# Linear attention and a gated feed-forward on one core: batch 0 by pairs of heads, its key products on two 64x64 tiles, and one transpose issued ahead of a load

## The chip, the cores and the metric

One core of one Trainium2 chip. The metric is device time in microseconds (us), the median of several executions. The profile gives a span of a little less: 284.0 us for an execution of the kernel before that was timed at 285.86 us.

## The reference

```python
q, k, v: (8 batches, 8 heads, 576 positions, 64) float32
q_s = softmax(q, over the 64)          k_s = softmax(k, over the 576 positions)
kv  = einsum('bhsd,bhse->bhde', k_s, v)            # 64x64 per head
x   = einsum('bhsd,bhde->bhse', q_s, kv)           # then (4608 tokens, 512)
h   = x @ w_in                                     # w_in  (512, 2048)
out = (h * sigmoid(beta * h)) @ w_out              # w_out (2048, 512)
```

The expert part (two products per token) is nearly all of TensorE's work. Attention is small, but the expert part of batch 0 can't begin before attention of batch 0 has delivered its transposed output, called XT below.

## The kernel before

The kernel records operations in one order; each engine runs its own in that order, and waits on semaphores only where data or a buffer demand it. So the place of an operation in the text is its place in its engine's queue. The eight heads go as four pairs (hp 0 to 3), two heads on 128 partitions. The 576 positions are cut in 512 (slabs t = 0 to 7, one for each batch) and 64 "remainders", which together make slab 8.

For a pair, the two heads' key exps lie on the diagonal of a block form (EK), zeros beside them, so that one 128-wide product serves both heads. Batch 0 before:

```python
def exp_kh(b, hp, n, e_):          # one head of n pairs: 64 partitions, ScalarE
    ... e.activation(o, a, ACT.Exp) ...
def ksum(b, hp, kb):               # 9 products, 1 column: the sums of key exps
    for j in range(NG):
        mm(PS[kb][:, hp:hp + 1], EK.., ones.., ...)
def kv_mm(b, hp, bk, n, w=D):      # 9 products, 64 or 65 columns: keys x values
    for j in range(NG):
        mm(PS[bk][:, VW * n:VW * n + w], EK.., VB.., ...)

load_main("qf", ...); load_k(0, 4)            # later: load_v(0, 4), then w_in
exp_q(0)
for hp in range(2):
    exp_kh(0, hp, 1, hp); exp_kh(0, hp, 1, 1 - hp)
exp_kh(0, 2, 2, 0); exp_kh(0, 2, 2, 1)        # pairs 2 and 3 together
...
cast_v(0, 0); cast_v(0, 1); cast_v(0, 2, ACTE); cast_v(0, 3)   # VB, default GpSimd
cast_win(0, 2, POOL); cast_win(0, 3, POOL); cast_win(1, 0, POOL)
...
out_now(0, 0, 0, ACTE)             # product QT x KVD, then the copy to XT (here ScalarE)
```

After the products come a reciprocal and two multiplies on VectorE (KVD, the normalised 64x64 blocks), one product with the transposed queries (QT) and the copy to XT. With XT, the first expert product starts: 64 matmuls "XT, WIN" for slab 0, then 64 "WOUT, GT".

`warm(...)` are filler products whose results nobody reads. The end of slab 0's work:

```python
                norm_rem(0)      # VectorE: query remainders of batches 0 and 1 normalised
                store(0)         # SyncE queue: output of slab 0
                load(3)          # SyncE queue: q, k, v of batch 3, query remainders of 2 and 3
                tr_dma(0)        # SyncE queue: DMA transpose EQR -> QTR
```

QTR is used in the second half of slab 1, by eight small products (remainders of batches 0 and 1).

The softmax here doesn't subtract the row's maximum and nothing guards it: scores larger than these inputs give would overflow.

Of the kernel before, what the change touches and what calls it, by code (L numbers as in the profile page):

```python
# [14 lines left out]
D = 64  # L15
# [28 lines left out]
class Program:  # L44
# [12 lines left out]
    def add(self, eng, fn, r=(), w=(), bank=(), slot=None, after=()):  # L57
        op = Op(eng, fn, slot)
        op.pos = len(self.ops)
        deps = op.deps  # L60
        deps.extend(after)
        for k in r:
            deps.extend(self.writer.get(k, ()))
            self.readers.setdefault(k, []).append(op)
        for k in w:
            for d in self.readers.get(k, ()):
                if d is not op and not self._same(d, op):
                    deps.append(d)
            for d in self.writer.get(k, ()):
                if not self._same(d, op):  # L70
                    deps.append(d)
            self.readers[k] = []
            self.writer[k] = [op]
        for k in bank:
            t = self.touch.setdefault(k, {})
            for e, d in t.items():
                if e != eng:
                    deps.append(d)
            t[eng] = op
        if eng == POOL and slot is None:  # L80
            if self.pool is not None:
                deps.append(self.pool)
            self.pool = op
        self.ops.append(op)
        return op
# [71 lines left out]
def bass_efficient_attn_shen__then__act_swish_beta_kernel(  # L157
# [12 lines left out]
    with ExitStack() as es:  # L170
# [57 lines left out]
        def homes_vk(i):  # L228
            add(POOL, lambda e: e.memset(VB[i][:, :, :, D:VW], 1.0), w=[("vone", i)])
            for e_ in range(2):  # L230
                z = KVD[i][64 * e_:64 * e_ + 64, :, 64 * (1 - e_):64 * (2 - e_)]
                add(POOL, lambda e, z=z: e.memset(z.bitcast(F32), 0.0), w=[("kvz", i, e_)])
# [36 lines left out]
        def load_k(b, split=1, cs=None, engs=(SP,)):  # L269
            load_pairs("kf", kt_h, KF, b, split, cs, engs)  # L270

        def load_v(b, split=1, cs=None):
            load_pairs("vf", vt_h, VF, b, split, cs)

        def load(b):
# [7 lines left out]
        load_main("qf", qt_h, QF, 0, 4, None, (SP, ACTE))  # L283
        add(ACTE, lambda e: e.dma_start(BT[:, :], bass.AP(beta_h, 0, [[512, 4], [1, 512]])),
            w=["bt"], slot="bt")
        load_k(0, 4)
        add(ACTE, lambda e: e.activation(DUMMY[:, 0:1], WARM[:, 0:1], ACT.Exp), r=["warm"],
            w=["dummy"])

# [20 lines left out]
        def exp_kh(b, hp, n, e_):  # L310
            i = b % 2
            o = bass.AP(EK[i], 64 * e_ * NHP * NG * 128 + hp * NG * 128 + 64 * e_,
                        [[NHP * NG * 128, 64], [128, NG * n], [1, 64]])
            a = bass.AP(KF[i], 64 * e_ * NHP * KW + hp * KW,
                        [[NHP * KW, 64], [64, NG * n], [1, 64]])
            hps = range(hp, hp + n)
            add(ACTE, lambda e: e.activation(o, a, ACT.Exp),  # L317
                r=[("kf", i, h) for h in hps], w=[("ek", i, h, e_) for h in hps])

        def exp_qr(pi):  # L320
            i = pi % 2
# [37 lines left out]
            rot[0] += 1  # L359
            return pool[rot[0] % len(pool)]  # L360

        def mm(o, l, r_, start, stop, r=(), w=(), bk=0, tr=False):
            if tr:
                add(PE, lambda e: e.transpose(o, l, r_), r=r, w=w, bank=[bk])  # L364
            else:
                add(PE, lambda e: e.matmul(o, l, r_, start=start, stop=stop), r=r, w=w, bank=[bk])  # L366

        def t_steps(b, hps, pool=MB, eng=DVE):
            i = b % 2
# [19 lines left out]
        def kv_rows(b, hp, j):  # L389
            i = b % 2  # L390
            return (EK[i][:, hp, j, :], VB[i][:, hp, j, :],
                    [("ek", i, hp, 0), ("ek", i, hp, 1), ("ekz", i, 0), ("ekz", i, 1)],
                    [("vb", i, hp, 0), ("vb", i, hp, 1)], [("vone", i)])
# [103 lines left out]
        def warm(n, bk, long=False):  # L497
            for _ in range(n):
                if long:
                    mm(PS[bk][:, :], bass.AP(XT8, 0, [[NM * SM, 128], [1, 256]]).bitcast(F32),  # L500
                       bass.AP(XT8, 0, [[NM * SM, 128], [1, 1024]]).bitcast(F32), True, True,
                       r=["xw"], w=[("ps", bk)], bk=bk)
                else:
                    mm(PS[bk][:, :], WARM[:, 0:128], WARM[:, :], True, True, r=["warm"],
                       w=[("ps", bk)], bk=bk)



        def ksum(b, hp, kb):
            for j in range(NG):  # L510
                l, r_, ke, kv, ko = kv_rows(b, hp, j)
                mm(PS[kb][:, hp:hp + 1], l, r_[:, D:D + 1], j == 0, j == NG - 1, r=ke + ko,
                   w=[("ps", kb)], bk=kb)

        def ksum_inv(b, kb, hp0, n, c0, step):
            i = b % 2
            s_ = bass.AP(PS[kb], c0, [[512, 128], [step, n]])
# [3 lines left out]
        def kv_mm(b, hp, bk, n, w=D):  # L521
            for j in range(NG):
                l, r_, ke, kv, ko = kv_rows(b, hp, j)
                mm(PS[bk][:, VW * n:VW * n + w], l, r_[:, 0:w], j == 0, j == NG - 1,
                   r=ke + kv + ko, w=[("ps", bk)], bk=bk)

        def out_now(b, hp, bk, eng):
            i = b % 2
# [31 lines left out]
        def load_win(c, m=0, nm=NM):  # L560
            a = bass.AP(win_h, m * 128 * DFF + 512 * c, [[DFF, 128], [128 * DFF, nm], [1, 512]])
            add(SP, lambda e: e.dma_start(STAGE[c][:, m:m + nm, :], a), w=SKEY[c][m:m + nm],
                slot=f"win{c}{m}")
# [27 lines left out]
        homes_ek(0, 0)  # L591
        homes_ek(0, 1)
        homes_vk(1)
        warm(3, 0, True)
        exp_q(0)
        for hp in range(2):
            exp_kh(0, hp, 1, hp)
            exp_kh(0, hp, 1, 1 - hp)
        exp_kh(0, 2, 2, 0)
        exp_kh(0, 2, 2, 1)  # L600
        norm_main(0, 0, 1)
        norm_main(0, 1, 1, POOL)
        go(t_steps(0, (0,), (3,)))
        turn_beta()
        warm(1, 0, True)
        norm_main(0, 2, 1, POOL)
        norm_main(0, 3, 1)
        go(t_steps(0, (1,), (4,)))
        ksum(0, 0, KB)
        load_v(0, 4)  # L610
        for c in range(4):
            for m in range(0, NM, 1 if c < 2 else 2):
                load_win(c, m, 1 if c < 2 else 2)
        cast_v(0, 0)
        cast_v(0, 1)
        cast_v(0, 2, ACTE)
        cast_v(0, 3)
        cast_win(0, 2, POOL)
        cast_win(0, 3, POOL)
        cast_win(1, 0, POOL)  # L620
        warm(1, 0, True)
        go(t_steps(0, (2,), (5,)))
        ksum(0, 1, KB)
        ksum_inv(0, KB, 0, 2, 0, 1)
        warm(1, 0)
        kv_mm(0, 0, 7, 0)
        kvd(0, 0, 7, 0)
        go(t_steps(0, (3,), (6,)))
        kv_mm(0, 1, 1, 0)
        kvd(0, 1, 1, 0)  # L630

        orot = [0]

# [27 lines left out]
                tick()  # L661

        FIRST = (16, 5)
        out_now(0, 0, 0, ACTE)
        cast_win(0, 0, DVE)
        kv_mm(0, 2, 7, 0, D + 1)
        ksum_inv(0, 7, 2, 1, D, 1)
        kvd(0, 2, 7, 0)
        cast_win(0, 1, DVE)
        out_now(0, 1, 6, ACTE)  # L670
        at = by_m(0, 0, 4)
        kv_mm(0, 3, 1, 0, D + 1)
        at(0)
        out_now(0, 2, 0, ACTE)
        ksum_inv(0, 1, 3, 1, D, 1)
        kvd(0, 3, 1, 0)
        at(1)
        out_now(0, 3, 7, DVE)
        read_beta()
        add(ACTE, lambda e: e.activation(DUMMY[:, 1:2], WARM[:, 0:1], ACT.Silu), r=["warm"],  # L680
            w=["dummy"])
# [72 lines left out]
        for t in range(NSLAB):  # L754
# [48 lines left out]
            if t == 0:  # L803
                load_qrem(0)
                load(2)
                scale_wout(0)
                scale_wout(4)
                exp_q(1, 0, 2)
                norm_main(1, 0, 1)
                scale_wout(8)  # L810
                norm_main(1, 1, 1, POOL)
                exp_q(1, 2, 2)
                exp_kh(1, 0, 2, 0)
                exp_kh(1, 0, 2, 1)
                norm_main(1, 2, 1, POOL)
                norm_main(1, 3, 1)
                scale_wout(12, 2)
                for hp in range(NHP):
                    cast_v(1, hp, POOL if hp else ACTE)
                pass2_group(0, (0, 1, 2, 3), (3, 4, 5, 6), tick)  # L820
                while todo:
                    todo.pop()[1]()
                at = by_m(1, 0, FIRST[1])
                o2_evac(0, 2, 5, ACTE)
                exp_qr(0)
                add(ACTE, lambda e: e.activation(DUMMY[:, 2:3], WARM[:, 0:1], ACT.Silu),
                    r=["warm"], w=["dummy"])
                at(0, 0, 3)
                out_now(1, 2, 7, DVE)
                at(1, 0, 3)  # L830
                go(kv_steps(1, (3,), (0,)))
                at(0, 3)
                at(1, 3)
                out_now(1, 3, 7, DVE)
                at(2)
                at(3)
                o2_evac(0, 3, 6, DVE)
                norm_rem(0)
                store(0)
                load(3)  # L840
                tr_dma(0)
                continue
            nb = [t + 2] if t + 2 < B else []
            if t == 1:
# [62 lines left out]
```

## Time and profile before

| | before |
|---|---|
| time | 285.6 us, median of 3 |
| span, TensorE busy | 284.0 us, 276.1 us (97%) |
| first expert product starts | 13.91 us |
| WOUT products start | 28.45 us |
| products on QTR start | 68.98 us |

First the view of TensorE's waits, kernel before. Columns: who waited and for whom, total us, how often, the longest.

```profile
PE PS L366 <- DVE XT L219: 1.5, 1, 1.5
PE PS L366 <- DMA QTR<-EQR: 1.1, 1, 1.1
PE PS L366 <- DVE KVD L403: 0.7, 1, 0.7
PE PS L366 <- DVE WOUT L555: 0.2, 1, 0.2
```

The first is the very beginning. The others are all the waits that this view lists in 284 us. The largest of them is for the transposed remainders. Its timeline (start, duration, engine, line, operation, tiles, count, idle before it and who ended that):

```profile
65.79 2.11 PE L366 MATMUL PS<-WOUT,GT 128*128 128x512 bf16 x8
68.98 0.26 PE L366 MATMUL PS<-QTR,KVD 128*128 128x64 bf16 x3 [1.09 <-DMA QTR<-EQR]
```

The SyncE queue of the same kernel, in order of time:

```profile
49.27 0.36 SPq L716 DMA_DIRECT2D out_dram<-O2S  x1
49.67 0.44 SPq L249 DMA_DIRECT2D QF<-in_q_dram  x1
...
53.58 6.86 SPq L266 DMA_DIRECT2D QRF<-in_q_dram  x2
60.48 3.98 SPq L456 DMA_TRANSPOSE QTR<-EQR  x1
```

VectorE had the remainders ready at 50.9 us, but the transpose is issued at 60.48, because load(3) is ahead of it: its last two issues alone hold the queue for 6.86 us. It lands 8.5 us after its issue, as the view by tile says:

```profile
DMA to landing us min/median/max: 8.5/8.5/8.5
```

The view of stretches, kernel before, says why it lands so late (the columns after the stretch are busy us and counts of each engine, then the granted clock, the share of the DMA engines, GB/s):

```profile
4.00:16.00 12.00, 11.33 (x98) 6.47 (x98) 9.49 (x27) 9.59 (x15) 6.72 (x11) 1.00 1.03 368
16.00:28.00 12.00, 11.94 (x56) 5.79 (x55) 5.90 (x17) 9.68 (x16) 2.97 (x4) 1.00 1.04 396
```

The DMA engines are full (share 1.0) in these stretches, as they are up to 64 us. A transfer issued then lands when those ahead of it have passed: all 95 transfers of the SyncE queue landed in their order of issue. And TensorE is nearly full too. The start, on which most of the change works, is this part of ScalarE's timeline:

```profile
7.41 4.90 ACT L317 ACTIVATE EK<-KF 64x576 bf16<-64x576 f32 x6 [0.90 <-DMA KF<-in_k_dram]
12.34 0.67 ACT L351 CAST VB<-VF 128x576 bf16<-128x576 f32 x1
12.92 0.58 ACT L530 CAST XT<-PS 128x512 bf16<-128x512 f32 x1
```

Key exps fill ScalarE from 7.4 to 12.3 us, and only then come the third V cast and the first copy of XT.

### The profile page before, as it was taken

How to read it: one execution, taken by the hardware profiler on the slowest of the kernel's cores; microseconds unless marked ns; L12 is line 12 of the kernel's file. 1: busy time of each engine (PE TensorE's matmuls, PEld its weight loads, DVE VectorE, ACT ScalarE, POOL GpSimd, SP SyncE). 2: the span in 40 equal slices, each digit the busy share in tenths (PEclk: the TensorE clock that was granted, in tenths of full speed). 3: DMA queues.
4: the chain of work that ended last, by engine and by line, in shares of the span. 5: the costliest groups of instructions: out<-in, count | busy, mean ns of one | idle time of the engine just before them, and what ended most of it. 6: DMA issues, size and time to landing. Idle time of an engine off the chain costs nothing.

```text
span 284.0 us, 3884 instructions
## 1 busy us (share of the span) xinstructions
PE 276.1 (97%) x1559; PEld 136.3 (48%) x1589; DVE 117.2 (41%) x218; ACT 178.9 (63%) x243; POOL 38.5 (14%) x57
## 2 busy tenths in 40 slices
PE   7999999998999999999999999999999999999995
PEld 3644454444455445544454445444554444444443
DVE  4864786126791248114741564054804300110012
ACT  5978688989867935796479737892660076018500
POOL 6522041127031122100140000000000000000000
PEclk9999999999999999999999999999999999999999
DMA  7999999999999998207980033002600030012022
GB/s 242 376 392 398 390 370 314 403 383 170 359 296 271 354 312 306 39 16 242 370 132 1 0 150 74 2 1 88 152 2 0 0 150 0 0 45 105 0 74 74
DMA packets 41466, 50.07 MB, mean 176 GB/s; under 512 B 20324, under 2 KB 28772, under 8 KB 40296
## 3 DMA queue, kind: packets, MB, share of 16 engines
q1 hardware_dynamic: 40496, 48.77, 54.3%
q10 hardware_dynamic: 952, 1.06, 1.1%
q8 instruction: 12, 0.20, 0.3%
q14 instruction: 6, 0.05, 0.0%
HBM read 36.71 MB, written 9.44 MB: 162 GB/s over the span
## 4 chain that ended last, share of the span: by engine, by line
PE 94%; DMA 3%; issue 1%; ACT 0%; DVE 0%
PE PS L366 93%; DMA QTR<-EQR 3%; PE PS L364 1%; ACT GT L642 0%; DVE XT L219 0%; DVE O2S L731 0%; DVE KVD L403 0%; ACT L295 0%
## 5 line engine op out<-in xcount | busy, mean ns | idle before, releaser
L642 ACT ACTIVATE GT<-PS,BETA 128x512 bf16<-128x512 f32 x144 | 96.8, 689 | 79.1 <-PE PS L366 79.1
L366 PE MATMUL PS<-WOUT,GT 128*128 128x512 bf16 (+2 forms) x579 | 131.4, 373 | 0.8 <-DVE WOUT L555 0.2
L366 PE MATMUL PS<-XT,WIN 128*128 128x512 bf16 x561 | 131.2, 379 | 0.5
L366 PEld LDWEIGHTS PS<-XT,WIN 128*128 128x128 bf16 x576 | 60.1, 106 | 59.3 <-POOL WIN L566 0.5
L366 PEld LDWEIGHTS PS<-WOUT,GT 128*128 128x128 bf16 x592 | 55.2, 98 | 62.3 <-ACT GT L642 0.4
L710 DVE COPY O2S<-PS 128x512 f32<-128x512 f32 x33 | 22.7, 687 | 107.7 <-PE PS L366 107.7
L366 PE MATMUL PS<-VB,EK 128*128 128x65 bf16 (+2 forms) x306 | 35.8, 191 | 1.0 <-DVE KVD L403 0.7
L351 POOL CAST VB<-VF 128x576 bf16<-128x576 f32 x30 | 22.7, 756 | 79.5 <-PE PS L366 49.9
L307 ACT ACTIVATE EK<-KF 64x1152 bf16<-64x1152 f32 x24 | 27.8, 1158 | 0.4
L332 DVE TENSOR_REDUCE QS<-EQ 128x8 f32<-128x512 bf16 (+1 forms) x22 | 20.1, 913 | 14.5 <-ACT EQ L295 14.4
L366 PEld LDWEIGHTS PS<-VB,EK 128*128 128x128 bf16 x306 | 22.0, 98 | 7.4 <-ACT VB L351 0.6
L441 DVE CAST XT<-PS 128x512 bf16<-128x512 f32 x24 | 16.4, 690 | 10.9 <-PE PS L366 10.9
L295 ACT ACTIVATE EQ<-QF 128x512 bf16<-128x512 f32 x32 | 17.9, 620 | 3.2 <-DMA QF<-in_q_dram 3.0
L334 DVE TENSOR_TENSOR EQ<-EQ,QI 128x1024 bf16<-128x1024 bf16 (+1 forms) x15 | 16.8, 1118 | 0.5
L366 PE MATMUL PS<-QT,KVD 128*128 128x512 bf16 x30 | 11.4, 380 | 0.0
L317 ACT ACTIVATE EK<-KF 64x576 bf16<-64x576 f32 (+1 forms) x12 | 9.9, 839 | 2.1 <-DMA KF<-in_k_dram 2.0
L334 POOL TENSOR_TENSOR EQ<-EQ,QI 128x512 bf16<-128x512 bf16 x7 | 7.3, 1042 | 16.3 <-DVE QI L333 16.0
L366 PE MATMUL PS<-XT 128*128 128x512 f32 x10 | 7.7, 908 | 1.5 <-DVE XT L219 1.5
L403 DVE TENSOR_TENSOR KVD<-PS,RC 64x64 bf16<-64x64 f32 (+2 forms) x28 | 8.6, 308 | 1.1 <-PE PS L364 0.2
L295 ACT ACT_TABLE_LOAD x6 | 7.7, 1283 | 0.1
L642 ACT ACT_TABLE_LOAD x5 | 6.4, 1283 | 0.1
L366 PE MATMUL PS<-QTR,KVD 128*128 128x64 bf16 x32 | 5.2, 193 | 1.1 <-DMA QTR<-EQR 1.1
(51 smaller groups left out, 74.3 us busy)
## 6 DMA issues: line engine op xcount, KB each, us to landing
out_dram<-O2S SPq DMA_DIRECT2D x8, 1024.0 KB, 4.2
KF<-in_k_dram SPq DMA_DIRECT2D x6, 1152.0 KB, 8.3
VF<-in_v_dram SPq DMA_DIRECT2D x6, 1152.0 KB, 10.7
QF<-in_q_dram SPq DMA_DIRECT2D x6, 1024.0 KB, 6.2
KF<-in_k_dram SPq DMA_DIRECT2D x8, 288.0 KB, 8.2
VF<-in_v_dram SPq DMA_DIRECT2D x8, 288.0 KB, 8.9
WST<-in_moe_w_in_dram SPq DMA_DIRECT2D x8, 256.0 KB, 8.2
O2S<-in_moe_w_in_dram SPq DMA_DIRECT2D x4, 512.0 KB, 11.7
```

The source lines that it names most:

```text
L295: add(ACTE, lambda e, o=o, a=a: e.activation(o, a, ACT.Exp), r=[("qf", i, hp)], w=[("eq", i, hp)])
L307: add(ACTE, lambda e, o=o, a=a: e.activation(o, a, ACT.Exp), r=[("kf", i, h) for h in hps], w=[("ek", i, h, e_) for h in hps])
L317: add(ACTE, lambda e: e.activation(o, a, ACT.Exp), r=[("kf", i, h) for h in hps], w=[("ek", i, h, e_) for h in hps])
L332: add(DVE, lambda e: e.tensor_reduce(s_, a, AX.X, ALU.add), r=ks, w=[("qs", i, hp0)])
L334: add(eng, lambda e: e.tensor_tensor(a, a, vb, ALU.mult), r=ks + [("qi", i, hp0)], w=ks)
L351: add(eng, lambda e: (e.copy if eng == ACTE else e.tensor_copy)(o, a), r=[("vf", i, hp), ("vone", i)], w=[("vb", i, hp, h) for h in ((0, 1 ...
L364: add(PE, lambda e: e.transpose(o, l, r_), r=r, w=w, bank=[bk])
L366: add(PE, lambda e: e.matmul(o, l, r_, start=start, stop=stop), r=r, w=w, bank=[bk])
L403: add(DVE, lambda e, o=o, a=a, s_=s_: e.tensor_tensor(o, a, s_, ALU.mult), r=[("ps", bk)] + [("rc", i, h) for h in hps], w=[("kvd", i, h, ...
L441: add(eng, lambda e: (e.copy if eng == ACTE else e.tensor_copy)(XT[i][:, hp, :], PS[bk][:, :]), r=[("ps", bk)], w=[("xt", i, hp)], bank=[bk])
L642: add(ACTE, lambda e: e.activation(GT[:, f, :], PS[bk][:, :], ACT.Silu, scale=BETA[:, f:f + 1]), r=[("ps", bk), "beta"], w=[("gt", f)], ba ...
L710: add(eng, lambda e: (e.copy if eng == ACTE else e.tensor_copy)(O2S[t % 2][:, u, :], PS[bk][:, :]), r=[("ps", bk)], w=[("o2", t % 2, u)], ...
```

## The change

There are two independent parts. The first, at the start: K and V of batch 0 are loaded pair by pair in turn. The key exps are kept compact, both heads of a pair in one operation on all 128 partitions, written to the still unused buffer GT. Instead of a block form, two products on separate 64x64 tiles of TensorE serve the two heads, and the sum of the exps comes as a 65th column. Casts move between engines to fit, and so does the normalising multiply of the queries of pair 3 (from VectorE to GpSimd; cut below). The second part is one line: the transpose of query remainders goes ahead of load(3).

```diff
-        load_k(0, 4)
+        for hp in range(NHP):
+            load_k(0, 4, (hp,))
+            load_v(0, 4, (hp,))
 ...
+        def exp_kc(hp):
+            o = bass.AP(GT, hp * KW, [[NF * SM, 128], [1, KW]])
+            a = bass.AP(KF[0], hp * KW, [[NHP * KW, 128], [1, KW]])
+            add(ACTE, lambda e: e.activation(o, a, ACT.Exp), r=[("kf", 0, hp)], w=[("ekc", hp)])
 ...
+        def kv_tiles(hp, bk):
+            for j in range(NG):
+                for e_ in range(2):
+                    p = slice(64 * e_, 64 * e_ + 64)
+                    mm(PS[bk][p, 0:D + 1],
+                       bass.AP(GT, 64 * e_ * NF * SM + hp * KW + j * D, [[NF * SM, 64], [1, D]]),
+                       VB[0][p, hp, j, 0:D + 1], j == 0, j == NG - 1,
+                       ..., bk=bk, tp=(64 * e_, 64 * e_))
+            ksum_inv(0, bk, hp, 1, D, 1)
+            kvd(0, hp, bk, 0)
 ...      # batch 0: ksum, kv_mm and exp_kh go (cut); the new order is
+        for hp in range(NHP):
+            exp_kc(hp)
+            if hp < 2:
+                cast_v(0, hp, ACTE)
 ...
+        cast_v(0, 2)
+        cast_v(0, 3, POOL, 1)            # 4 of 9 blocks on GpSimd
+        cast_win(0, 1, POOL)
         cast_win(0, 2, POOL)
-        cast_win(0, 3, POOL)
         cast_win(1, 0, POOL)
 ...
+        kv_tiles(1, 1)
+        out_now(0, 0, 0, ACTE)
         go(t_steps(0, (3,), (6,)))
+        warm(1, 3)
+        out_now(0, 1, 5, ACTE)
+        kv_tiles(2, 7)
+        cast_v(0, 3, ACTE, 0)            # the other 5 blocks on ScalarE
+        cast_win(0, 0, DVE)
+        warm(1, 3)
+        kv_tiles(3, 1)
+        out_now(0, 2, 0, ACTE)
 ...
         at = by_m(0, 0, 4)               # at(m): four XT,WIN products
         at(0)
+        out_now(0, 3, 7, DVE)
         at(1)
-        out_now(0, 3, 7, DVE)
+        cast_win(0, 3, DVE)
 ...
                 store(0)
+                tr_dma(0)
                 load(3)
-                tr_dma(0)
```

## The prediction

> What bounds it now. TensorE is the long chain: the page gives PE 276.1 us busy of a 284.0 us span, and the chain of waits is 94% PE. 1,152 large products at 0.2155 us from start to start (timeline) are 248 us; some 36 us are start-up, attention and stalls. The view of waits names four PE stalls: 1.5 us at the start, 0.7 at 12.8 (KVD), 0.2 at 40.15 (WOUT), 1.1 at 68.98 (QTR). But a second limit lies under the first 68 us: the stretches show DMA at share 1.0 and 350 to 410 GB/s from 4 to 64 us. The last w_in piece lands at 24.95, its cast ends at 25.7, and some 12 products (2.6 us) follow: the first expert product cannot end before about 28.0; it ends at 28.45 now. WOUT f=8 lands at 34.08; from there VectorE is full (scale, three reductions, a multiply ending at 39.47, scale of f=12), so PE cannot pass f=12 before about 39.9; it does at 40.15.
>
> What the change does.
> 1. Loads K0 V0 K1 V1 ... instead of K0-3 V0-3. Same bytes and queue: V0 lands near 8.1 instead of 10.4, V3 at 12.6 and w_in at 13.2 to 24.95 as before.
> 2. Key exps: six ScalarE operations, 4.9 us, become four of 128x576, about 0.67 us each (as a 128x576 cast there), 2.7 us; the last still waits for K3 (11.9).
> 3. 18 key-sum and 36 product instructions go; 72 products on 64x64 tiles come. Nine 128-wide ones took 0.30 us of issue. The Trainium skill, "TensorEngine Tiling (Array Packing)", says under Key Properties that tiles run in parallel but a mode switch drains the array, and under Restrictions that column tiling disables Fast Weight Load; no trace of before shows either. My estimate is 0.55 to 0.9 us per pair, against about 0.45 now: 0.5 to 1.8 us more PE work at the start.
> 4. Casts of w_in are redistributed, c=0 m=3 onto VectorE behind the last XT copy. Following VB3, KVD, output, XT3 and that cast, I get the first sweep (f 0 to 3) ending at 18.4 to 19.5, against 18.0.
> Earlier attention cannot buy much: w_in caps the gain at 0.45 us, f=12 at 0.25 us. Some 0.3 us of delay is swallowed there. Net at 40 us: -0.2 to +0.8, centre +0.2.
> 5. The transpose of query remainders is ready at 50.9 (VectorE's multiply ends) but sits in the SyncE queue behind load(3): issued 60.48, landed 68.94. Ahead of it, it should be issued near 51 and land near 58 to 60; PE wants it at 67.9. The 1.09 us stall goes. What PE needs next is there: EK of batch 2 ends at 68.5, wanted about 69.5; QT lands about 70, wanted 71.2. No PE wait is listed after, so this gain should reach the end.
>
> Sum: 285.6 - 1.1 + 0.2 = 284.7 us; 8 in 10 between 283.7 and 285.9. Faster by over 2% (5.7 us): 1%; within 2%: 98%; slower by over 2%: 1%.
>
> Right if: the QTR wait disappears and its landing is near 59; w_in landings are unchanged; PE begins the WOUT products at 28.0 to 29.5; idle before f=12 grows if the start got faster, vanishes if slower. Wrong if w_in or WOUT landings move by over 0.5 us, or tile products take over 1 us per pair.
>
> What would make it wrong: tile products much cheaper or dearer; PE gaps at 13 to 16 us lowering the granted clock; the early transpose opening a hole in the DMA stream, so that batch 2 or 3 comes late; a new wait for EK or QT at 69 us eating the 1.1 us.

## The result, and the profile after

All outputs are right. 284.81 us (284.76 to 284.93, 4 runs) against 285.46 us (285.14 to 286.05, 4 runs). The ratio is 0.9975, with a 95% interval of 0.9958 to 0.9993. Ratios are taken from the fast runs of both kernels in the same rounds, so they are not quite the ratio of the medians quoted. The span is 283.1 us.

TensorE's waits, kernel after:

```profile
PE PS L373 <- DVE XT L219: 1.5, 1, 1.5
PE PS L373 <- ACT VB L358: 0.4, 1, 0.4
PE PS L373 <- DVE KVD L411: 0.3, 1, 0.3
```

The wait for QTR is gone, and no new one stands in its place. The second and third are both in the start. TensorE's timeline around the QTR products and the SyncE queue, kernel after:

```profile
65.71 2.54 PE L373 MATMUL PS<-WOUT,GT 128*128 128x512 bf16 x11
68.08 0.25 PE L373 MATMUL PS<-QTR,KVD 128*128 128x64 bf16 x3
```

```profile
49.62 0.36 SPq L719 DMA_DIRECT2D out_dram<-O2S  x1
51.30 1.50 SPq L464 DMA_TRANSPOSE QTR<-EQR  x1
```

```profile
DMA to landing us min/median/max: 6.5/6.5/6.5
```

Issued at 51.30 and landed 6.5 us later, at 57.8, the transpose is ready 10 us before it is wanted. The last product before it starts at 67.52 before, and the QTR products 1.46 us later instead of the 0.2157 us that a 512-column product takes from start to start: a gap of 1.25 us went.

Now the start: ScalarE's timeline, kernel after.

```profile
11.50 0.68 ACT L325 ACTIVATE GT<-KF 128x576 bf16<-128x576 f32 x1 [0.82 <-DMA KF<-in_k_dram]
12.09 0.57 ACT L544 CAST XT<-PS 128x512 bf16<-128x512 f32 x1
13.07 0.59 ACT L544 CAST XT<-PS 128x512 bf16<-128x512 f32 x1 [0.41 <-PE PS L373]
13.55 0.46 ACT L358 CAST VB<-VF 128x320 bf16<-128x320 f32 x1
```

The last of the four exps is shown. One operation on 128 partitions takes 0.68 us, and the six of before, one head each or one head of two pairs, took 4.90. The first XT copy is at 12.09 instead of 12.92. So the attention of the first pairs is earlier; yet the first expert product comes later. TensorE's timeline around it, before and then after:

```profile
13.07 0.46 PE L366 MATMUL PS<-VB,EK 128*128 128x65 bf16 x9 [0.67 <-DVE KVD L403]
...
13.59 0.45 PE L366 MATMUL PS<-VB,EK 128*128 128x65 bf16 x9
13.91 1.02 PE L366 MATMUL PS<-XT,WIN 128*128 128x512 bf16 x4
```

```profile
12.64 0.39 PE L373 MATMUL PS<-QT,KVD 128*128 128x512 bf16 x1 [0.33 <-DVE KVD L411]
12.96 0.47 PE L373 MATMUL PS<-VB,GT 64*64 64x65 bf16 x18
13.37 0.39 PE L373 MATMUL PS<-WARM 128*128 128x512 bf16 x1
14.16 0.47 PE L373 MATMUL PS<-VB,GT 64*64 64x65 bf16 x18 [0.40 <-ACT VB L358]
14.56 0.39 PE L373 MATMUL PS<-QT,KVD 128*128 128x512 bf16 x1
14.99 1.04 PE L373 MATMUL PS<-XT,WIN 128*128 128x512 bf16 x4
```

Before, the last pair's products begin at 13.59 and the expert products at 13.91. After, they begin at 14.16, behind the ScalarE half of the V cast, and at 14.99. The WOUT products start at 29.03 instead of 28.45. Later comes the second part's gain, and the last TensorE product starts at 279.92 instead of 280.83.

| start of (us) | before | after | difference |
|---|---|---|---|
| first XT,WIN product | 13.91 | 14.99 | +1.08 |
| WOUT products of slab 0 | 28.45 | 29.03 | +0.58 |
| first key-value product of batch 1 | 40.58 | 40.93 | +0.35 |
| QTR products | 68.98 | 68.08 | -0.90 |
| last TensorE product | 280.83 | 279.92 | -0.91 |

The sum is visible: +0.35 at 40 us, -1.25 at 69 us, -0.90 to the end. These are two single executions: that of before was timed at 285.86 us, 0.40 over its median, and the medians differ by 0.65 us, not by 0.90.

Half of the 1.08 us is made up before the WOUT products, and most of that is seen in the traces: in the kernel after, one product of attention stands among the 64 XT,WIN products where before two did (0.22 us), and none of them comes late, where before one came 0.17 us late at 17.12.

### The profile page after: what moved, and what is told of

It is laid out like the page before. It is cut to its first block, busy times and chain, and to the rows that moved or that the text cites. A ratio compares the mean times of both kernels' runs of the same rounds, so it can differ in the third digit from the quotient of the medians.

```text
span 283.1 us, 3950 instructions
## 1 busy us (share of the span) xinstructions
PE 277.9 (98%) x1608; PEld 136.3 (48%) x1608; DVE 117.0 (41%) x218; ACT 177.6 (63%) x243; POOL 38.1 (13%) x57
## 4 chain that ended last, share of the span: by engine, by line
PE 98%; DVE 0%; ACT 0%; issue 0%
PE PS L373 97%; PE PS L371 1%; ACT XT L544 0%; DVE XT L219 0%; DVE KVD L411 0%; ACT VB L358 0%; DVE O2S L734 0%; DVE RC L520 0%
## 5 line engine op out<-in xcount | busy, mean ns | idle before, releaser
L373 PE MATMUL PS<-WOUT,GT 128*128 128x512 bf16 (+2 forms) x592 | 132.8, 373 | 0.0
L373 PE MATMUL PS<-VB,EK 128*128 128x65 bf16 x252 | 33.3, 193 | 0.0
L358 POOL CAST VB<-VF 128x576 bf16<-128x576 f32 (+1 forms) x29 | 21.1, 729 | 77.9 <-DMA VF<-in_v_dram 73.5
L373 PEld LDWEIGHTS PS<-VB,EK 128*128 128x128 bf16 x252 | 20.0, 98 | 6.5
L341 DVE TENSOR_TENSOR EQ<-EQ,QI 128x1024 bf16<-128x1024 bf16 (+1 forms) x14 | 15.9, 1132 | 0.5
L373 PE MATMUL PS<-QT,KVD 128*128 128x512 bf16 x32 | 12.2, 380 | 0.3 <-DVE KVD L411 0.3
L341 POOL TENSOR_TENSOR EQ<-EQ,QI 128x512 bf16<-128x512 bf16 x8 | 8.3, 1042 | 17.3 <-DVE QI L340 17.0
L432 DVE RECIPROCAL RC<-PS 128x4 f32<-128x4 f32 (+2 forms) x9 | 1.6, 177 | 10.0 <-PE PS L373 9.9
L319 ACT ACTIVATE EK<-KF 64x576 bf16<-64x576 f32 (+1 forms) x6 | 5.0, 842 | 1.0 <-DMA KF<-in_k_dram 0.9
```

Of the source, the lines that this page charges most:

```text
L319: add(ACTE, lambda e: e.activation(o, a, ACT.Exp), r=[("kf", i, h) for h in hps], w=[("ek", i, h, e_) for h in hps])
L341: add(eng, lambda e: e.tensor_tensor(a, a, vb, ALU.mult), r=ks + [("qi", i, hp0)], w=ks)
L358: add(eng, lambda e: (e.copy if eng == ACTE else e.tensor_copy)(o, a), r=[("vf", i, hp), ("vone", i)], w=[("vb", i, hp, h) for h in ((0, 1 ...
L373: add(PE, lambda e: e.matmul(o, l, r_, start=start, stop=stop, tile_position=tp), r=r, w=w, bank=[bk])
```

## The experiments

Theory: the one-line turn brings the whole gain; the new start costs some of it, through waits on ScalarE and VectorE and a little more TensorE work. Rivals: the new start brings the gain; or the tiles themselves (mode switches) are what makes the start late. Experiments of one call ran on one chip and share the runs of the kernel before. All had five rounds. Medians of before were 285.3 (first four), 285.27 (next four) and 285.26 us (last three).

### turn_alone: before, with the turn only

```diff
                 store(0)
+                tr_dma(0)
                 load(3)
-                tr_dma(0)
```

> The kernel before with one edit: the transpose of query remainders issued ahead of the load of batch 3. Theory (the gain of the whole change is this alone, and the new start costs time): the QTR wait of TensorE at 69 us goes, about 1.2 us off the time of before (ratio about 0.9957), that is about 0.35 us faster than the whole change. The WOUT products still begin at 28.4 to 28.5. Rival (the new start brings the gain, and the turned order only lets the wait reappear as another one): within 0.3 us of before.

Measured: 284.3 us, ratio 0.9962 (0.9945 to 0.9979). The view of its waits has one line left, the very beginning:

```profile
PE PS L366 <- DVE XT L219: 1.5, 1, 1.5
```

The WOUT products start at 28.40, as in before, and the QTR products at 67.45. One line of code gives at least what the whole change did; that it gives more is shown below, where both ran on one chip. The first theory holds, and the rival falls.

### start_alone: the whole change, the turn undone

```diff
                 store(0)
-                tr_dma(0)
                 load(3)
+                tr_dma(0)
```

> The whole change without the turned order: the transpose back behind the load of batch 3. Theory: the WOUT products begin at about 29.0 instead of 28.45, 0.2 us of that is swallowed before f=12 at 40 us, and the QTR wait at 69 us is back, only less deep (about 0.7 to 0.9 us instead of 1.1), because its landing is set by the DMA queue and TensorE arrives later. So the time is within 0.3 us of before (ratio 0.999 to 1.001). Rival: the new start alone is 0.5 us or more faster than before (ratio under 0.9983).

Measured: 285.58 us, ratio 1.0005 (0.9989 to 1.0021): no gain. TensorE's waits, this kernel, without the first line (the very beginning):

```profile
PE PS L373 <- ACT VB L358: 0.4, 1, 0.4
PE PS L373 <- DVE KVD L411: 0.3, 1, 0.3
PE PS L373 <- DMA QTR<-EQR: 0.3, 1, 0.3
PE PS L373 <- DVE WIN L580: 0.2, 1, 0.2
```

The WOUT products start at 29.14. The QTR wait is back, but only 0.3 us by this view (0.46 us from start to start, against 1.25; I had expected 0.7 to 0.9). Of the 0.79 us less, 0.46 is TensorE coming later (the product ahead starts at 67.97 instead of 67.52), and 0.33 is that the transpose landed at 68.60 instead of 68.94, with nearly the same issue (60.30 and 60.48), which the edit does not explain. So the old wait hides most of the new start's delay: that is why this kernel is hardly slower than before (0.28 us by the medians, within the noise), and why the two parts' effects can't be added up.

### turn_f12: turn_alone, with the stop before f=12 taken away (a miss)

The kernel before also stops at 40.15 us, for WOUT f=12, which VectorE scales only after a multiply for batch 1. This edit moves that multiply to GpSimd, and the transposes of batch 1 that needed it behind f=12.

```diff
-                norm_main(1, 3, 1)
+                norm_main(1, 3, 1, POOL)
                 scale_wout(12, 2)
 ...
-                (112, lambda: go(t_steps(1, (2, 3), (2,), ACTE))),
-                (112.1, lambda: (scale_wout(14, 2), exp_kh(1, 2, 1, 0), exp_kh(1, 2, 1, 1))),
-                (115, lambda: kv_mm(1, 0, 0, 0, D + 1)), (117, kv1),
+                (112.1, lambda: scale_wout(14, 2)),
+                (115, lambda: kv_mm(1, 0, 0, 0, D + 1)),
+                (116, lambda: go(t_steps(1, (2, 3), (2,), ACTE))),
+                (116.1, lambda: (exp_kh(1, 2, 1, 0), exp_kh(1, 2, 1, 1))), (117, kv1),
```

> turn_alone, and beside it the stop before f=12 at 40 us is taken away: the multiply of head pair 3 of batch 1 goes to GpSimd, so that VectorE scales WOUT f=12 at once when it lands (38.4), and the eight transposes that stood ahead of f=12 come after the first key-value products. Theory (that stop is a floor set by VectorE, and hides 0.3 us of anything gained earlier): f=12 begins at 39.2 to 39.5 instead of 40.15, and the time is 0.3 to 0.6 us under turn_alone. Rival (WOUT f=14 and 15, which land at 40.5 and 41.2, are the real floor): less than 0.15 us under turn_alone, with a new wait for WOUT at 41 to 42 us.

Measured: 284.58 us, ratio 0.9975 (0.9958 to 0.9993). No gain, and neither theory nor rival described it. The trace of turn_alone tells why: there the stop isn't there. Its WOUT f=8 landed at 33.77 us instead of 34.08, f=12 at 37.95 instead of 38.37, and from 38 to 42 us no TensorE product started over 0.04 us late. The stop that I took from the single trace of before comes and goes with a few tenths in the landing of loads; over the thirteen traces the f=8 landing lies between 33.53 and 34.29. In turn_f12, f=12 came at once, but the next products then waited 0.19 us for a V cast of batch 1, and the QTR products started at 67.46, as in turn_alone.

### wide: the whole change, but block form and 128-wide products

```diff
         for hp in range(NHP):
-            exp_kc(hp)
+            exp_kh(0, hp, 1, 0)
+            exp_kh(0, hp, 1, 1)
 ...
         def kv_tiles(hp, bk):
-            for j in range(NG): ... two tiles ...
+            kv_mm(0, hp, bk, 0, D + 1)
             ksum_inv(0, bk, hp, 1, D, 1)
             kvd(0, hp, bk, 0)
```

> The whole change, but the key exps of batch 0 in the block form of before (two ScalarE operations of 64 rows per pair) and 128-wide products instead of the 64x64 tiles. Theory (what the tiles buy is ScalarE time: four operations of 0.68 us less; on TensorE they cost about 0.1 us per pair): XT of pair 0 is copied at about 13.3 instead of 12.1, the last V cast ends about 0.9 us later, the WOUT products begin at 29.6 to 30.0, and the time is 0.6 to 1.0 us over the whole change. Rival (mode switches and tile products on TensorE are what delays the new start): the WOUT products begin earlier than 29.0, and the time is not longer than that of the whole change.

Measured: 287.63 us, ratio 1.008 (1.0061 to 1.0098). By the medians it is 2.3 us over before of the same rounds and 2.8 us over the 284.81 us of the whole change, about three times what I expected. TensorE's timeline, and two stretches (same columns as above), this kernel:

```profile
13.02 0.38 PE L373 MATMUL PS<-WARM 128*128 128x512 bf16 x1
15.62 0.65 PE L373 MATMUL PS<-VB,EK 128*128 128x65 bf16 x9 [2.23 <-ACT VB L358]
```

```profile
14.00:16.00 2.00, 0.38 (x8) 0.41 (x9) 0.62 (x1) 1.45 (x3) 0.96 (x2) 0.80 1.03 356
16.00:18.00 2.00, 2.00 (x10) 0.83 (x9) 0.61 (x3) 1.24 (x2) 0.61 (x1) 0.50 1.05 404
```

The direction is the theory's. ScalarE's longer exps delay the last V cast by 1.5 us, to 15.02 to 15.48. The size was off for a reason that I had not foreseen: TensorE stood idle for 2.23 us, and the clock was then granted at 0.50 from 15.18 to 18.60 us, so the products that followed ran at half speed. The WOUT products start at 31.57, 2.54 us later than in the whole change. An estimate: half of the 2.97 us from 15.62 to 18.60, 1.5 us, is the clock, and the other 1.0 us is the delay that the theory was about. All five executions show a mean clock of 0.993 or 0.994, so all of them lost it.

This run also prices the tiles on TensorE, since the same products stand at the same places. A pair takes 0.29 us wide (first to last start and one step), and 0.41 us from the first of 18 tile products to the next instruction of another kind; the entry into tile mode costs another 0.09 us (from a QT product to tile products 0.320 us, to wide ones 0.226 us). So the tiles cost about 0.2 us more per pair, of which two times 0.09 are the entry and exit. They buy ScalarE time, 0.68 us per pair.

### v3_pool: the whole change, VB3 whole on GpSimd

```diff
-        cast_v(0, 3, POOL, 1)
+        cast_v(0, 3, POOL)
 ...
-        cast_v(0, 3, ACTE, 0)
```

> The whole change, but the V cast of pair 3 whole on GpSimd, where VB3 is free by 12.9 instead of 14.1; the other half no longer stands on ScalarE behind the XT copy of pair 1. Theory A (the wait for VB3 at 14.16, the last one that the view of TensorE's waits names, delays the start): the first w_in products begin by about 14.4 instead of 14.99 and the WOUT products near 28.5. Theory B (VectorE's order ends the wait: the cast of w_in c=0 m=0, landed at 13.1, stands behind the KVD multiplies of pair 2 and runs 14.5 to 14.9): the first w_in products stay at about 15.0, the WOUT products at about 29.0, and the time within 0.1% of the whole change. I hold B.

Measured: 284.94 us, ratio 0.9988 (0.9975 to 1.0001). The tile products of pair 3 start at 13.55 instead of 14.16, but the first expert product is at 15.13 and WOUT at 29.17. Theory B: VectorE's timeline of this kernel shows the cast of w_in behind the multiplies of pair 2,

```profile
13.86 0.47 DVE L411 TENSOR_TENSOR KVD<-PS,RC 64x64 bf16<-64x64 f32 x2
14.37 0.71 DVE L580 CAST WIN<-WST 128x512 bf16<-128x512 f32 x1
```

though that piece of w_in had landed at 13.45. Taking away the largest wait that the list names for the start gave nothing, because another wait ends just behind it.

### start2: the start put in order

```diff
-        cast_v(0, 3, POOL, 1)
+        cast_v(0, 3, POOL)
 ...
+        cast_win(0, 0, DVE)
         kv_tiles(2, 7)
-        cast_v(0, 3, ACTE, 0)
-        cast_win(0, 0, DVE)
-        warm(1, 3)
         kv_tiles(3, 1)
-        out_now(0, 2, 0, ACTE)
 ...                                       # the warm(1, 3) ahead of out_now(0, 1) stays
         at(0)
-        out_now(0, 3, 7, DVE)
+        out_now(0, 2, 0, ACTE)
         at(1)
         cast_win(0, 3, DVE)
+        out_now(0, 3, 7, DVE)
```

(The text speaks of two short filler products; only one was taken out.)

> The whole change, with VB3 whole on GpSimd, the cast of w_in c=0 m=0 ahead of the KVD multiplies of pair 2 on VectorE, the cast of c=0 m=3 ahead of the copy of XT3, the output of pair 2 after the first four w_in products, and without two short filler products. Theory (the new start is late by waits for what VectorE and ScalarE do in the wrong order, not by the tiles): the first w_in products at 13.6 to 14.0, the WOUT products at 28.0 to 28.5, time about that of turn_alone (ratio to before 0.9945 to 0.9965). Rival (mode switches and tile products set it): WOUT products still at 28.8 or later.

Measured: 284.27 us, ratio 0.9971 (0.9959 to 0.9983). TensorE's timeline, this kernel:

```profile
13.01 0.76 PE L373 MATMUL PS<-VB,GT 64*64 64x65 bf16 x36
13.82 1.02 PE L373 MATMUL PS<-XT,WIN 128*128 128x512 bf16 x4
```

The WOUT products start at 28.16. The tiles are still there, and the delay isn't: it was the order of the work (casts, outputs and one filler), not the tiles.

### start3: start2 without the second long filler

```diff
         go(t_steps(0, (1,), (4,)))
-        warm(1, 0, True)
         cast_v(0, 2)
```

> start2 without the second long filler product (1.1 us of TensorE between the transposes of pairs 1 and 2). Theory (the landing of w_in is a floor): although attention is ready up to 1 us earlier, the WOUT products begin no earlier than 27.6, gaps appear in front of w_in products between 20 and 26 us, and the time is at most 0.3 us under start2. Rival (no floor there): WOUT products begin at 27.0 to 27.4 and the time is 0.6 us or more under start2. A granted clock under 1.0 in the first 15 us would be a third outcome, from the missing filler.

Measured: 284.26 us, ratio 0.9969 (0.9957 to 0.9981). The products of pair 2 start at 12.38 instead of 13.01, yet the first expert product is at 13.88 and WOUT at 28.22: nothing gained. The time is as the theory had it, but not its reason. There is no gap ahead of any w_in product between 20 and 26 us. The floor is earlier, and it is in the loads:

```profile
12.50 0.67 POOL L358 CAST VB<-VF 128x576 bf16<-128x576 f32 x1 [0.78 <-DMA VF<-in_v_dram]
13.22 0.47 PE L373 MATMUL PS<-VB,GT 64*64 64x65 bf16 x18 [0.36 <-POOL VB L358]
13.31 0.43 DVE L580 CAST WIN<-WST 128x512 bf16<-128x512 f32 x1 [0.85 <-DMA WST<-in_moe_w_in_dram]
```

V of the last pair and the first piece of w_in are both used within 0.05 us of their landing (12.44 and 13.28), and the clock stayed at 1.0. The second is the floor, and more than this kernel stands on it: in the six traces of turn_alone, turn_f12, turn_again, start2, start3 and start2_again, the first expert product starts 0.60 us after the landing of the first w_in piece, the time of its cast and of the way to TensorE. In the kernel before it was 0.68 us (13.23 and 13.91). So a new start that keeps this load and this cast had only about 0.1 us to gain at that product.

### loads_alone: before, with only the loads in turn

```diff
-        load_k(0, 4)
+        for hp in range(NHP):
+            load_k(0, 4, (hp,))
+            load_v(0, 4, (hp,))
 ...
-        load_v(0, 4)
```

> The kernel before with the loads of batch 0 in turn (K0 V0 K1 V1 ...) and nothing else. Theory (the turn pays only with exps by pair: K3 now lands at 11.9 instead of 9.6, and ScalarE's exps of pairs 2 and 3 together wait for it): those exps end near 14.2 instead of 12.3, the copy of XT0 moves from 12.9 to about 15, the WOUT products begin at 29.8 to 30.8, and since the QTR wait at 69 us takes up to 1.1 us of it, the time is 0.5 to 1.3 us over before. Rival (earlier V is worth something by itself): the time is not over that of before.

Measured: 286.27 us, ratio 1.0048 (1.0026 to 1.007). ScalarE's timeline and one line of TensorE's, this kernel:

```profile
11.69 2.35 ACT L319 ACTIVATE EK<-KF 64x1152 bf16<-64x1152 f32 x2 [1.68 <-DMA KF<-in_k_dram]
14.06 0.67 ACT L353 CAST VB<-VF 128x576 bf16<-128x576 f32 x1
14.79 0.46 PE L368 MATMUL PS<-VB,EK 128*128 128x65 bf16 x9 [2.44 <-ACT VB L353]
```

As the theory said, ScalarE waits for K3 and the exps of pairs 2 and 3 end near 14. TensorE waited 2.44 us for that V cast, and in the profiled execution the clock fell to 0.5 here too, from 15.62 to 19.03, so that its WOUT products start at 31.69, 0.9 us later than the latest I had allowed. But that execution (287.57 us) is not the usual one. Two of the six show a mean clock of 0.993 and took 287.57 and 287.80 us; the other four show 0.999 or 1.000 and took 285.74 to 286.39, which is 0.5 to 1.1 us over the median of before, as forecast. So here the clock is lost in some executions only; what the four did in the start no trace shows. The turned loads need the exps by pair.

### after_again, turn_again, start2_again: the three on one chip

The three kernels were repeated unchanged, so there is no diff.

> The whole change once more, beside the two below on one chip. Theory (the turned transpose brings the gain and the new start costs some of it): ratio to before 0.9975 to 0.9985.

> turn_alone once more. Theory: 0.3 to 0.6 us under the whole change in the same rounds (ratio to before 0.9955 to 0.997). If it is not faster than the whole change here, the cost of the new start is not shown by times, only by the traces.

> start2 once more. Theory: within 0.2 us of turn_again, because the first w_in products begin within 0.2 us of each other and neither trace has a wait of over 0.25 us behind them; and 0.3 us or more under the whole change.

| same rounds | median us | ratio to before | first XT,WIN | WOUT | QTR |
|---|---|---|---|---|---|
| the whole change | 285.02 | 0.9993 (0.9976 to 1.0011) | 15.06 | 29.10 | 68.16 |
| the turn alone | 284.28 | 0.9968 (0.9951 to 0.9985) | 13.86 | 28.29 | 67.34 |
| start2 (with the turn) | 284.35 | 0.9970 (0.9954 to 0.9986) | 13.78 | 28.11 | 67.50 |

The turn alone is 0.74 us under the whole change by the medians, a little more than I expected; its slowest run (284.69) is under the fastest of the whole change (284.82). Here the whole change measured 0.9993, just outside the 0.9975 to 0.9985: its interval in these rounds includes 1, and the earlier one lay just under 1. start2 and the turn alone can't be told apart.

## Why the prediction was right

**The sum.** 284.7 predicted, 284.81 measured, in the range. The two terms were -1.1 and +0.2. By the first two traces they were -1.25 and +0.35; by medians of the same rounds the turn is worth 1.0 us (both times), and the new start on top of it costs 0.74. Both signs are right, and the start's cost was put too low. That the total came within 0.11 us is partly luck: the repeat gave 285.02, only 0.24 us under before of its rounds, and the range held the 285.46 us of before as well. What tests the prediction is its steps.

**Step 5, the turn: right.** Issued at 51.30 and landed at 57.8 (58 to 60 was said), the wait gone, no new wait behind it. turn_alone shows it by itself: ratio 0.9962. The term was sized from the listed wait of 1.09 us, which counts from the modelled end of the product before; from start to start it was 1.25 us.

**Step 4, the start late: right, with the cause only partly foreseen.** The last product of the first sweep (f 0 to 3) started at 18.45 and the next one at 18.67 (18.4 to 19.5 was said), WOUT began at 29.03 (28.0 to 29.5). start2 shows that the cause lies in the order of casts on ScalarE, GpSimd and VectorE, the place of the outputs and one filler; v3_pool shows that the VB3 cast alone isn't. Which of start2's other edits was needed wasn't tried one by one.

**Step 3, the tiles: a little cheaper than said.** The estimate was 0.55 to 0.9 us per pair, measured 0.50 (0.41 and 0.09 for the entry). The Trainium skill, "TensorEngine Tiling (Array Packing)", Key Properties, says that different tiles execute in parallel and that changing the mode drains TensorE. The trace agrees with both: the products of the two tiles mostly start 3 to 4 ns apart, and pair follows pair every 32 ns, as one wide product follows another in wide; each change of mode costs 0.09 us, which fits a drain.

**Steps 1 and 2: right, but for a test that was too sharp.** V0 landed at 7.67 (8.1 was said), the last w_in piece at 24.45 (24.95 was said; exactly at the edge of the half microsecond I had allowed, but over the thirteen traces told of here it lies between 24.39 and 25.14, and between 24.39 and 24.95 for the start of before alone, so this half microsecond can't be put down to the change). The WOUT landings moved a little further: f=8 came at 33.55 instead of 34.08, 0.53 us, and over 0.5 us was a sign of being wrong. It is no sign: turn_again, with the start of before, has 33.58. One compact exp took 0.68 us (0.67 was said).

**The floors: one of the two moves from run to run.** "PE cannot pass f=12 before about 39.9" was true of the one trace that I had. turn_alone and turn_again, with the same start as before, passed without a stop; start2_again, which comes to that place a little earlier with f=8 landed at 33.85, stopped for 0.3 us in all. So "some 0.3 us of delay is swallowed there" depends on how the loads of an execution happen to land. That agrees with the start costing 0.35 us between the first two traces and 0.71 us between the traces of after_again and turn_again (last TensorE product at 280.00 and 279.28), as the medians of the same rounds have it. The floor at 28.0 us from the last w_in piece was neither confirmed nor refuted: start3 was held by the landing of the first w_in piece before it could reach it (28.22 us). That earlier floor the prediction did not name.

**Named as a risk, and near:** a lower clock from gaps at 13 to 16 us. In the whole change the gaps of TensorE are 0.5 and 0.6 us, and the clock stays. In wide, with a wait of 2.2 us in its trace, it fell in all five executions; in loads_alone, with 2.4 us in its trace, in two of six. Even of before, one execution in nine beside turn_alone shows a mean clock of 0.994 and took 286.35 us; where it lost it no trace shows.

## What to carry to other kernels

When the DMA engines are full, ask what stands ahead in the queue (here the order of issue was the order of landing): put a transfer that somebody waits for ahead of others that nobody wants yet. One line of this kind gave all of the gain here. A rebuilt start gave none of it: its order of casts, outputs and filler brought the first expert product late, and put in order it was no faster than the old start, because the landing of w_in was a floor under both. Test the parts of a change singly, and where two waits lie one behind the other, expect nothing from removing one, and distrust a stop of a few tenths that only one trace shows.

## What the Trainium skill lacked or had wrong

- "TensorE: Matmul & The Clock Gate" (Part 1) gives at least one idle window of about 3.4 us as what throttles the clock again. Here less was enough. In wide the granted clock fell to 0.5 at 15.18, and TensorE had been idle for 1.9 of the 3.41 us before that (the wait of 2.23 us began at 13.4). In loads_alone it fell at 15.62, after 2.44 us of idle in the 3.41 us before (12.35 to 14.79); this is one of the two executions, of six, that lost it. That the slow stretch then lasts about one window agrees: 3.41 us in both.
- "TensorEngine Tiling (Array Packing)" (Key Properties) says that a change of tiling mode drains TensorE but gives no cost. Here it is 0.09 us on entry and 0.09 us on exit; nine pairs of 64x64 products with 65 columns took 0.41 us with the exit, nine 128-wide ones 0.29 us.
- "DMA: Bandwidth & Descriptors" has no figure for a DMA transpose behind a full queue. Here it took 8.3 to 8.9 us from issue to landing behind a load (three traces), 4.5 to 7.5 us ahead of it (ten traces).
